# A decode step on one core: TensorE loops tile by tile, and the softmax runs in groups of six and two blocks

## The chip, the cores and the metric

One core of one Trainium2 chip. The time is the device time of one execution, in microseconds (us), as the median of several runs. The kernel before ran at 1293.13 us (three runs, 1293.12 to 1293.23). The profile is one execution, with its own span of 1291.9 us. The time does not start and end with the profile's span and is 1.3 to 1.5 us longer, so spans are compared with spans and times with times.

## The reference

One step of attention over a long cache, plus a small MLP, for 8 sequences:

```python
q = (xn @ wq)                          # xn = layernorm(x): 8 x 576; 32 heads of 128
scores = einsum(q, k_cache) * 128**-0.5   # k_cache, v_cache: 8 x 32 x 4096 x 128, bf16
o = einsum(softmax(scores), v_cache) @ wo
h = gelu(layernorm(xn) @ w1 + b1)      # 576 -> 4608
out = x + o + h @ w2 + b2
```

The two caches are 268 MB each and every byte is used once. Everything else together is about 20 MB.

## The kernel before

The caches pass through a ring in SBUF in 32 tiles. A tile is 128 partitions: eight heads of one sequence, 16 partitions a head, 256 keys in each partition. One tile has one key load and one value load of 8.39 MB each, both issued by SyncE on one queue:

```python
for t in range(1, NT):
    sy.wait_ge(sem["kf"], 2 * t - 1)   # TensorE has read enough of the old keys
    load_kv(k_v, t, 0)
    sy.wait_ge(sem["vf"], t)           # TensorE has read the old values
    load_kv(v_v, t, 1)
```

VectorE multiplies each of eight key blocks by the query in place, TensorE adds up groups of 16 columns with identity matmuls, and VectorE reduces the rest to scores. The softmax is done in two halves of four blocks. `spread_heads` turns the exponentials into matmul weights `ebd`:

```python
def vector_tile(t, u):
    ve.wait_ge(sem["k"], 16 * (u + 1))
    for x in range(NX):                     # NX = 8 blocks
        ...                                 # product of block x, in place
        if x > 1:
            reduce(u, x - 2)
        if x == NCB + 2:                    # after product 6
            spread_heads(u, 0)              # first half of the softmax
    reduce(u, NX - 2)
    reduce(u, NX - 1)
    spread_heads(u, 1)                      # second half
    ...                                     # reciprocal, scaling, result
```

TensorE's program has two tiles written out in one loop of 16 turns (64 product matmuls, 64 value matmuls, two totals, four transposes of the result in each tile); the first of the totals signals `vf`:

```python
with nc.Fori(0, NT // 2, 1, engines=[ENG.DVE, ENG.PE, ENG.Activation]) as it:
    for u in range(2):
        vector_tile(2 * it + u, u)
        tensor_tile(u)
        scalar_tile(u)
```

The softmax here doesn't subtract the row's maximum and nothing guards it: scores larger than these inputs give would overflow.

## Time and profile before

| | kernel before |
|---|---|
| time | 1293.13 us |
| HBM bytes read | 556.94 MB |
| from one load's completion to the next, steady | 19.35 us (433.5 GB/s) |
| a tile (two loads) | 38.70 us, without change |
| TensorE, VectorE busy | 60%, 64% |

The first excerpt is from the page of the kernel before. The row `DMA` is the busy share of the 16 DMA engines in 40 slices of the span, in tenths; the queue lines (`q1`, `q8`) give packets, MB and their share of the engines' time; the group lines give busy time and the mean of one instruction in ns, then the engine's idle time just before them and what ended it; the last two lines give the number of issues and the median time from issue to landing.

```profile
PE 770.1 (60%) x4780; PEld 318.3 (25%) x4780; DVE 828.1 (64%) x708; ACT 56.6 (4%) x181; POOL 1.4 (0%) x11
...
DMA  9999999999999999999999999999999999999998
...
q1 hardware_dynamic: 10368, 556.93, 99.7%
q8 instruction: 4, 0.07, 0.0%
...
DMA 82%; PE 11%; DVE 6%; issue 0%; ACT 0%; DVEq 0%; SPq 0%
...
L524 DVE TENSOR_TENSOR ring<-ring,qb 128x4096 bf16<-128x4096 bf16 x256 | 579.8, 2286 | 239.6 <-DMA ring<-in_A_k_cache_dram 239.3
...
ring<-in_A_k_cache_dram SPq DMA_DIRECT2D x32, 32.2
ring<-in_A_v_cache_dram SPq DMA_DIRECT2D x32, 29.4
```

Read it from the DMA row: it is 9 nearly throughout, while no compute engine is above 64%. A load takes 19.35 us on the wire but 32.2 or 29.4 us from issue to landing, so each one waits 10 to 13 us in the queue behind the one before. That is what a full queue looks like.

The next excerpt is the chain of waits of the kernel before: start, length, what.

```profile
556.52 32.16 DMA ring<-in_A_k_cache_dram
...
588.83 2.30 DVE ring L524
...
591.18 4.04 PE s_ps L552 x9
...
595.23 32.15 DMA ring<-in_A_k_cache_dram
```

The chain runs through the key load and then through 2.3 us of VectorE and 4 us of TensorE before the next key load is issued. This looks like 6 us of compute per tile on the path (the page sums it to 17%), but it is not: the load issued at 595.2 us only joins a queue in which the value load is still being moved. The chain follows the releaser of each step; it does not know that the DMA engines were busy with something else meanwhile. The completion times of the packets do: they come 19.35 us apart with no hole.

The excerpt is the timeline of the end of one tile in the kernel before (start, length, engine, line, operation, tiles, and in brackets the idle time before it); weight loads are left out.

```profile
571.87 1.29 DVE L506 TENSOR_REDUCE sc<-s_ps 128x32 f32<-128x512 f32 x2
...
573.85 1.91 PE L563 MATMUL o_ps<-ring,ebd 128*32 128x512 bf16 x32
...
575.11 1.23 DVE L514 TENSOR_TENSOR ebd<-e,head 128x1024 bf16<-128x1024 bf16 x1 [0.47 <-ACT e L582]
...
576.39 1.91 PE L563 MATMUL o_ps<-ring,ebd 128*32 128x512 bf16 x32 [0.64 <-DVE ebd L514]
...
578.65 0.33 SPq L246 DMA_DIRECT2D ring<-in_A_v_cache_dram  x1
...
580.49 0.19 DVE L541 TENSOR_TENSOR Ox<-on,quad 128x32 bf16 x1
588.83 2.29 DVE L524 TENSOR_TENSOR ring<-ring,qb 128x4096 bf16<-128x4096 bf16 x1 [8.15 <-DMA ring<-in_A_k_cache_dram]
```

The last product has ended at 571.9 us. The second half of the softmax follows (reduce, exp, spread), then the second half of the value matmuls, and the value load is released at 578.65 us. The tile's work ends at 580.7 us, and VectorE then waits 8.15 us for the next keys.

### The profile page before, as it was taken

The page shows a single profiled execution, that of the slowest core. Times are in us where ns is not written, and L with a number is a line of the kernel's source. Part 1 is how long each engine was busy: PE and PEld are TensorE (multiplying, and loading weights), DVE is VectorE, ACT ScalarE, POOL GpSimd, SP SyncE. Part 2 cuts the span into 40 slices and gives each one's busy share as a digit, 9 for nine tenths or more (in the row PEclk, how much of TensorE's full clock was granted, in tenths as well). Part 3 has the DMA queues.
Part 4 walks back from the last instruction along what each step waited for, and adds up shares of the span by engine and source line. Part 5 has one row for each costly group of instructions (what it writes and reads, how often), then busy time and mean ns, then how long its engine had stood idle before and what let it go on. Part 6 is the DMA issues. An engine that isn't in the chain of part 4 may idle for free.

```text
span 1291.9 us, 10994 instructions
## 1 busy us (share of the span) xinstructions
PE 770.1 (60%) x4780; PEld 318.3 (25%) x4780; DVE 828.1 (64%) x708; ACT 56.6 (4%) x181; POOL 1.4 (0%) x11
## 2 busy tenths in 40 slices
PE   5665675655665654675565575555565655675567
PEld 1122222222221222222222222222222222222223
DVE  2655677655677655677655677655677655577654
ACT  2100000000000000000000000000000000000000
POOL 0000000000000000000000000000000000000000
PEclk9877887777887777887778887777887777887779
DMA  9999999999999999999999999999999999999998
GB/s 415 445 425 443 428 428 444 426 428 446 424 430 444 426 432 442 426 432 440 428 442 428 428 444 426 428 446 424 430 444 428 430 442 426 432 440 428 442 428 352
DMA packets 10411, 557.03 MB, mean 431 GB/s; under 512 B 1163, under 2 KB 1188, under 8 KB 1446
## 3 DMA queue, kind: packets, MB, share of 16 engines
q1 hardware_dynamic: 10368, 556.93, 99.7%
q8 instruction: 4, 0.07, 0.0%
q10 hardware_dynamic: 38, 0.02, 0.0%
q14 instruction: 1, 0.01, 0.0%
HBM read 556.94 MB, written 0.01 MB: 431 GB/s over the span
## 4 chain that ended last, share of the span: by engine, by line
DMA 82%; PE 11%; DVE 6%; issue 0%; ACT 0%; DVEq 0%; SPq 0%
DMA ring<-in_A_k_cache_dram 77%; PE s_ps L552 10%; DVE ring L524 6%; DMA ring<-in_A_wo_dram 2%; DMA ring<-in_B_w_dram 2%; PE o_ps L387 1%; PE s_ps L387 1%; DVEq L524 0%; PE acc L347 0%; ACT L401 0%; DVE ring L404 0%; ACT ring L401 0%; DVE ring L402 0%; DVE ring L400 0%; ACT ring L397 0%
## 5 line engine op out<-in xcount | busy, mean ns | idle before, releaser
L552 PE MATMUL s_ps<-ring,ident 128*128 128x512 bf16 x2048 | 555.3, 429 | 477.5 <-DVE ring L524 476.6
L524 DVE TENSOR_TENSOR ring<-ring,qb 128x4096 bf16<-128x4096 bf16 x256 | 579.8, 2286 | 239.6 <-DMA ring<-in_A_k_cache_dram 239.3
L552 PEld LDWEIGHTS s_ps<-ring,ident 128*128 128x128 bf16 x2048 | 205.9, 107 | 808.8 <-DVE ring L524 549.5
L506 DVE TENSOR_REDUCE sc<-s_ps 128x32 f32<-128x512 f32 x256 | 173.1, 687 | 37.8 <-PE s_ps L552 37.8
L563 PE MATMUL o_ps<-ring,ebd 128*32 128x512 bf16 x2048 | 129.9, 401 | 13.5 <-DVE ebd L514 13.4
L514 DVE TENSOR_TENSOR ebd<-e,head 128x1024 bf16<-128x1024 bf16 x64 | 78.2, 1223 | 15.0 <-ACT e L582 15.0
L563 PEld LDWEIGHTS o_ps<-ring,ebd 128*32 128x32 bf16 x2048 | 50.9, 101 | 95.5 <-issue 30.7
L582 ACT ACTIVATE e<-sc 128x128 bf16<-128x128 f32 x64 | 19.9, 311 | 1080.2 <-DVE sc L506 1080.2
L535 DVE RECIPROCAL rec<-tot_ps 128x8 f32<-128x8 f32 x32 | 6.7, 208 | 82.1 <-PE tot_ps L569 82.1
L575 PE MATMUL oT_ps<-selc,ob 128*128 128x8 f32 x256 | 33.9, 259 | 5.2 <-ACT ob L586 5.2
L575 PEld LDWEIGHTS oT_ps<-selc,ob 128*128 128x128 f32 x256 | 31.0, 191 | 8.1 <-ACT ob L586 8.1
L538 DVE TENSOR_TENSOR on<-oT_ps,rec 128x8 bf16<-128x8 f32 x32 | 5.3, 167 | 34.7 <-PE oT_ps L575 34.7
L586 ACT ACTIVATE ob<-o_ps 128x512 f32<-128x512 f32 x32 | 19.1, 597 | 105.5 <-PE o_ps L563 105.5
L569 PEld LDWEIGHTS tot_ps<-headf,Ep 128*128 128x128 f32 x128 | 16.6, 188 | 13.6 <-issue 13.6
L569 PE MATMUL tot_ps<-headf,Ep 128*128 128x8 f32 x128 | 19.6, 261 | 0.0
L398 DVE TENSOR_SCALAR ring<-ring 96x384 f32<-96x384 f32 x2 | 0.7, 353 | 25.8 <-ACT ring L397 25.8
L582 ACT ACTIVATION_READ_ACCUMULATOR e<-sc 128x1 f32 x64 | 12.0, 187 | 0.0
L387 PE MATMUL o_ps<-ring 128*32 128x384 bf16 x27 | 7.9, 862 | 2.4 <-DMA ring<-in_B_w_dram 2.4
L541 DVE TENSOR_TENSOR Ox<-on,quad 128x32 bf16 x32 | 6.2, 193 | 4.8
L387 PE MATMUL s_ps<-ring 128*32 128x384 bf16 x27 | 7.9, 863 | 0.0
L347 PE MATMUL acc<-ring,hT_sb 128*8 128x288 bf16 x72 | 6.4, 350 | 1.7 <-DMA ring<-in_B_w_dram 1.7
L295 PE MATMUL tot_ps<-ident,ring 8*128 8x8 bf16 x9 | 0.7, 198 | 8.9 <-DVE ring L288 8.9
(77 smaller groups left out, 58.0 us busy)
## 6 DMA issues: line engine op xcount, KB each, us to landing
ring<-in_B_w_dram SPq DMA_DIRECT2D x2, 5184.0 KB, 25.4
ring<-in_A_wq_dram SPq DMA_DIRECT2D x1, 4608.0 KB, 13.8
ring<-in_A_wo_dram SPq DMA_DIRECT2D x1, 1728.0 KB, 28.9
ring<-in_A_wo_dram SPq DMA_DIRECT2D x1, 1584.0 KB, 28.9
ring<-in_A_wo_dram SPq DMA_DIRECT2D x1, 1008.0 KB, 30.9
ring<-in_A_k_cache_dram SPq DMA_DIRECT2D x32, 32.2
ring<-in_A_v_cache_dram SPq DMA_DIRECT2D x32, 29.4
ring<-in_A_wo_dram SPq DMA_DIRECT2D x1, 288.0 KB, 31.1
```

The lines of the kernel that those rows point to most:

```text
L347: i = e.matmul(acc[m][m * OP:m * OP + B, :ND], lhsT=lhsT, rhs=rhs[:, m * ND:(m + 1) * ND], start=start, stop=stop)
L387: i = e.matmul(h_ps[j][s * MP:(s + 1) * MP], lhsT=lhsT, rhs=wv[:, r0:r0 + HK, :], **flags)
L506: ins = ve.tensor_reduce(out=sc[i][:, n * CB:(n + 1) * CB], in_=bank_of(x).rearrange("p (c d) -> p c d", d=DL), axis=AX.X, op=ALU.add)
L514: ve.tensor_tensor(out=ebd[i][:], in0=es[i][:].rearrange("p (j c) -> p j c", c=4).unsqueeze(2).to_broadcast([P, J, G, 4]), in1=head[:].uns ...
L524: ve.tensor_tensor(out=k, in0=k, in1=qb[:, bass.ds(t, 1), :].to_broadcast([P, CB, Dh]), op=ALU.mult,).then_inc(sem["prod"], 1)
L535: ve.reciprocal(out=rec[:], in_=tot_ps[:, :G]).then_inc(sem["rec"], 1)
L552: ins = te.matmul(bank_of(x).rearrange("p (c d) -> p c d", d=DL), lhsT=idn, rhs=k[:, :, d * DL:(d + 1) * DL], start=(d == 0), stop=(d == n ...
L563: ins = te.matmul(o_ps[m * MP:(m + 1) * MP, :], lhsT=ebd[i][:, j].rearrange("p g c -> p (g c)"), rhs=ring_v[u][i][:, 4 * j:4 * j + 4, :], ...
L569: ins = te.matmul(tot_ps[:, :G], lhsT=Ep[:, i:i + 1].to_broadcast([P, P]), rhs=headf[:], start=(i == 0), stop=(i == 1))
L575: ins = te.matmul(oT_ps[:, :G], lhsT=ob[:, c, :], rhs=selc[:, c, :], start=(c == 0), stop=(c == 3))
L582: sa.activation(out=es[i][:], in_=sc[i][:], func=ACT.Exp, scale=scale, accum_out=Ep[:, i:i + 1]).then_inc(sem["x"], 1)
L586: sa.activation(out=ob[:].rearrange("r c d -> r (c d)"), in_=o_ps, func=ACT.Copy).then_inc(sem["ob"], 1)
```

## The change

Its intent, in its author's words: TensorE loops tile by tile, with two product sections and one values section, so that its program is 1021 instructions; and the softmax runs in groups of six and two blocks. The core of the diff (cuts marked):

```diff
-    HALVES = [(1, 0), (0, 1)]
+    BLOCKS = [(7, 0, 1, 2, 5, 6, 3, 4), (0, 1, 2, 5, 6, 7, 3, 4)]
+    LATE = 2
+    groups = [(0, NX - LATE), (NX - LATE, NX)]
 ...
         for x in range(NX):
+            if x == NX - 1:
+                reduce(u, x - 2)
 ...                                        # product of block x
-            if x > 1:
+            if 1 < x < NX - 1:
                 reduce(u, x - 2)
-            if x == NCB + 2:
-                spread_heads(u, 0)
+        spread_heads(u, 0)
         reduce(u, NX - 2)
         reduce(u, NX - 1)
         spread_heads(u, 1)
 ...
-    with nc.Fori(0, NT // 2, 1, engines=[ENG.DVE, ENG.PE, ENG.Activation]) as it:
+    with nc.Fori(0, NT // 2, 1, engines=[ENG.DVE, ENG.Activation]) as it:
 ...
+    block("even")
+    nc.regs_mov(odd, 0)
+    products(0)
+    te.br("values")
+    block("odd")
+    nc.regs_mov(odd, 1)
+    products(1)
+    te.br("values")
+    block("values")
 ...                                        # 64 value matmuls, one total, four transposes
+    turn_end(te, prod=NX, v=16, ebd=2, ob=1)
+    te.br_lt(odd, 1, on_true="odd", on_false="turn")
+    block("turn")
+    nc.regs_alu(turns, turns, 1, op=ALU.add)
+    te.br_lt(turns, NT // 2, on_true="even", on_false="project")
```

Besides this, the two small transposes of the head are merged into one of nine matmuls, and VectorE adds the two rows of softmax totals so that one totals matmul is left per tile. The bytes moved and the point at which key blocks are released do not change.

More of the change, by code (lines that the diff above doesn't have):

```diff
@@ L36, in __init__ @@
         self.sems, self.counts, self.seen, self.bufs = {}, {}, {}, {}
+        self.aside = []
     def buf(self, key):
@@ L49, in wait @@
         if self.seen.get((eng, sem.num), 0) < value:
-            getattr(self.nc, eng).wait_ge(sem, value)
             self.seen[eng, sem.num] = value
+            if eng == "tensor":
+                self.aside.append(lambda: self.nc.tensor.wait_ge(sem, value))
+            else:
+                getattr(self.nc, eng).wait_ge(sem, value)
     def deps(self, eng, reads, writes):
@@ L67, in op @@
             self.wait(eng, token)
-        ins = emit(getattr(self.nc, eng))
         if sem is None:
@@ L71, in op @@
             self.counts[eng] += 1
-            value = self.counts[eng]
-            ins.then_inc(sem, 1)
-            token = (eng, (sem, value))
+            token = (eng, (sem, self.counts[eng]))
         else:
-            ins.then_inc(sem, 16)
             token = ("dma", (sem, 16))
+        if eng == "tensor":
+            self.aside.append(lambda: emit(self.nc.tensor).then_inc(sem, 1))
+        else:
+            ins = emit(getattr(self.nc, eng))
+            ins.then_inc(sem, 1 if token[0] == eng else 16)
+            self.name = ins.ins.name
         for key in reads:
@@ L82, in op @@
             b.writer, b.readers = token, []
-        self.name = ins.ins.name
         return token[1]
@@ L106, in ahead, with later @@
     bb.instructions = rest[:at] + moved + rest[at:]
+def later(src, dst, engine):
+    ins = list(src.instructions)
+    wait = next(i for i in ins if i.engine == engine and type(i).__name__ == "InstEventSemaphore")
+    assert not dst.instructions
+    src.instructions = [i for i in ins if i is not wait]
+    dst.instructions = [wait]
 def decode(nc, A_x, A_k_cache, A_v_cache, A_wq, A_wo, B_x, B_w1, B_b1, B_w2, B_b2, out):
@@ L155, in decode @@
     qb = sb("qb", [P, NT, Dh], BF16)
-    ebd = [sb(f"ebd{i}", [P, J, G, 4], BF16) for i in range(2)]
-    sc = [sb(f"sc{i}", [P, CH], FP32) for i in range(2)]
-    es = [sb(f"e{i}", [P, CH], BF16) for i in range(2)]
+    ebd = sb("ebd", [P, 2 * J, G, 4], BF16)
+    sc = sb("sc", [P, C], FP32)
+    es = sb("es", [P, C], BF16)
     Ep = sb("Ep", [P, 2], FP32)
+    Es = sb("Es", [P, 1], FP32)
     ob = sb("ob", [P, 4, Dh], FP32)
@@ L207, in decode @@
     xn8, y8 = early(0, [B, D]), early(0, [B, D])
-    dup = early(0, [B, D, 2])
+    YP = 32
+    dup = early(0, [YP + B, D, 2])
     xT = early(0, [P, WC, MP])
@@ L226, in decode, with block @@
     od = Order(nc)
+    main = nc.cur_bb
+    def block(name, eng=ENG.PE):
+        nc.enter_bb(name, parent=main, valid_engines=[eng])
     wq_sb = ring[:, 0:WQ_END].rearrange("p (c f) -> p c f", c=WC)
@@ L258, in decode @@
     od.op("gpsimd", [], ["eps"], lambda e: e.memset(eps_col[:], EPS))
+    od.op("gpsimd", [], ["dup"], lambda e: e.memset(dup, 0.0))
     od.op("gpsimd", [], ["xT"], lambda e: e.memset(xT, 0.0))
@@ L285, in layernorm, with spread @@
             op0=ALU.subtract, op1=ALU.mult))
-    def spread(src, skey, dst, dkey, ps, pkey):
+    def spread(src, skey, p0):
         dve([skey], ["dup"], lambda e: e.tensor_copy(
-            out=dup, in_=src.unsqueeze(2).to_broadcast([B, D, 2])))
-        dupv = dup.rearrange("b d v -> b (d v)").rearrange("b (p c) -> b c p", c=WC)
-        tp = ps[:, :WC * B].rearrange("p (c b) -> p c b", c=WC)
-        def turn(e):
-            for c in range(WC):
-                i = e.matmul(
-                    tp[:, c, :], lhsT=dupv[:, c, :], rhs=ident[:B, :B], start=True, stop=True)
-            return i
-        pe(["dup", "ident"], [pkey], turn)
-        for v in range(2):
-            dve([pkey, "par"], [dkey], lambda e: e.tensor_tensor(
-                out=dst[:, :, v * B:(v + 1) * B], in0=tp,
-                in1=par[:, :, v:v + 1].to_broadcast([P, WC, B]), op=ALU.mult))
+            out=dup[p0:p0 + B], in_=src.unsqueeze(2).to_broadcast([B, D, 2])))
     layernorm(x8, "x8", xn8, "xn8", "x")
@@ L313, in decode, with turn_both @@
             in_=par2[:, 1 - v:2 - v].unsqueeze(1).to_broadcast([P, WC // 2, 1])))
-    spread(xn8, "xn8", xT, "xT", tot_ps, "tot")
+    spread(xn8, "xn8", 0)
     layernorm(xn8, "xn8", y8, "y8", "y")
-    spread(y8, "y8", yT, "yT", oT_ps, "oT")
+    spread(y8, "y8", YP)
     idn = ident[:]
+    dupv = dup.rearrange("b d v -> b (d v)").rearrange("b (p c) -> b c p", c=WC)
+    tp = tot_ps[:, :WC * 2 * B].rearrange("p (c t b) -> p c t b", c=WC, t=2)
+    two = idn[:YP + B, :2 * YP].rearrange("p (t i) -> p t i", t=2)[:, :, :B]
+    def turn_both(e):
+        for c in range(WC):
+            i = e.matmul(tp[:, c], lhsT=dupv[:, c, :], rhs=two, start=True, stop=True)
+        return i
+    pe(["dup", "ident"], ["tot"], turn_both)
+    for t, (dst, dkey) in enumerate(((xT, "xT"), (yT, "yT"))):
+        for v in range(2):
+            dve(["tot", "par"], [dkey], lambda e: e.tensor_tensor(
+                out=dst[:, :, v * B:(v + 1) * B], in0=tp[:, :, t],
+                in1=par[:, :, v:v + 1].to_broadcast([P, WC, B]), op=ALU.mult))
     act(["ident"], ["sel"], lambda e: e.activation(
@@ L362, in decode, with broadcast @@
         t = ps.rearrange("p (g d) -> p g d", d=Dh)
-        def broadcast(e):
+        def broadcast(e, t=t, b=b):
             for v in range(2):
@@ L391, in decode @@
     for c in range(WC):
-        pe(["yT", "w1"], ["h_ps"], lambda e: layer(
+        pe(["yT", "w1"], ["h_ps"], lambda e, c=c: layer(
             e, yT[:, c, :], w1_sb[:, c, :], start=(c == 0), stop=False))
@@ L408, in decode, with turn @@
         t = S_ps[j][:, :HK * HS * MP].rearrange("p (k n) -> p k n", k=HK)
-        def turn(e):
+        def turn(e, h=h, t=t):
             for k in range(HK):
@@ L454, in decode @@
         sy.dma_start(out=wo_rows(r0, r1), in_=wo_v[:, r0 * D:r1 * D]).then_inc(wo_in[-1], 16)
-    HALVES = [(1, 0), (0, 1)]
-    def block(u, x):
-        i, n = divmod(x, NCB)
-        return HALVES[u][i], (n + NCB - 1) % NCB if u == 0 and i == 0 else n
+    BLOCKS = [(7, 0, 1, 2, 5, 6, 3, 4), (0, 1, 2, 5, 6, 7, 3, 4)]
+    SLOTS = BLOCKS[1]
+    LATE = 2
+    assert len(SLOTS) == NX and all(b[-LATE:] == SLOTS[-LATE:] for b in BLOCKS)
+    groups = [(0, NX - LATE), (NX - LATE, NX)]
     def keys(u, x):
-        h, n = block(u, x)
-        at = home(u, 0) + h * CHUNK + n * BLOCK
+        at = home(u, 0) + BLOCKS[u][x] * BLOCK
         return ring[:, at:at + BLOCK].rearrange("p (c d) -> p c d", d=Dh)
-    ring_v = [[ring[:, h * CHUNK:(h + 1) * CHUNK].rearrange("p (c d) -> p c d", d=Dh)
-               for h in HALVES[u]] for u in range(2)]
+    vals = ring[:, :TILE].rearrange("p (c d) -> p c d", d=Dh)
     def bank_of(x):
@@ L500, in decode, with turn_end @@
         od.wait("tensor", od.last(e))
+    def turn_end(e, **counts):
+        for name, n in counts.items():
+            e.wait_ge(sem[name], n).then_inc(sem[name], -n)
     def reduce(u, x):
-        i, m = divmod(x, NCB)
-        n = block(u, x)[1]
+        n = SLOTS.index(BLOCKS[u][x])
         ve.wait_ge(sem["s"], NX * u + x + 1)
         ins = ve.tensor_reduce(
-            out=sc[i][:, n * CB:(n + 1) * CB],
+            out=sc[:, n * CB:(n + 1) * CB],
             in_=bank_of(x).rearrange("p (c d) -> p c d", d=DL), axis=AX.X, op=ALU.add)
-        if m == NCB - 1:
+        if x + 1 in (groups[0][1], NX):
             ins.then_inc(sem["sc"], 1)
     def spread_heads(u, i):
+        a, b = (n * CB for n in groups[i])
+        ja, jb, nj = a // 4, b // 4, (b - a) // 4
         ve.wait_ge(sem["x"], 2 * u + i + 1)
+        if i:
+            ve.tensor_tensor(out=Es[:], in0=Ep[:, 0:1], in1=Ep[:, 1:2], op=ALU.add)
         ve.tensor_tensor(
-            out=ebd[i][:],
-            in0=es[i][:].rearrange("p (j c) -> p j c", c=4).unsqueeze(2).to_broadcast([P, J, G, 4]),
-            in1=head[:].unsqueeze(1).unsqueeze(3).to_broadcast([P, J, G, 4]), op=ALU.mult,
+            out=ebd[:, ja:jb],
+            in0=es[:, a:b].rearrange("p (j c) -> p j c", c=4).unsqueeze(2)
+            .to_broadcast([P, nj, G, 4]),
+            in1=head[:].unsqueeze(1).unsqueeze(3).to_broadcast([P, nj, G, 4]), op=ALU.mult,
         ).then_inc(sem["ebd"], 1)
@@ L533, in vector_tile @@
         spread_heads(u, 1)
-        ve.wait_ge(sem["t"], 2 * u + 1)
+        ve.wait_ge(sem["t"], u + 1)
         ve.reciprocal(out=rec[:], in_=tot_ps[:, :G]).then_inc(sem["rec"], 1)
         ve.wait_ge(sem["rec"], 2 * u + 1)
-        ve.wait_ge(sem["t"], 2 * u + 2)
         ve.tensor_tensor(
@@ L544, in vector_tile, with scalar_tile, products @@
             in1=quad[:].unsqueeze(1).to_broadcast([P, G, M]), op=ALU.mult).then_inc(sem["on"], 1)
-    def tensor_tile(u):
+    def scalar_tile(u):
+        for i, (a, b) in enumerate(groups):
+            sa.wait_ge(sem["sc"], 2 * u + i + 1)
+            sa.activation(
+                out=es[:, a * CB:b * CB], in_=sc[:, a * CB:b * CB], func=ACT.Exp, scale=scale,
+                accum_out=Ep[:, i:i + 1]).then_inc(sem["x"], 1)
+        sa.wait_ge(sem["o"], u + 1)
+        sa.activation(
+            out=ob[:].rearrange("r c d -> r (c d)"), in_=o_ps, func=ACT.Copy
+        ).then_inc(sem["ob"], 1)
+    te.br("head")
+    assert NT % 2 == 0
+    with nc.Fori(0, NT // 2, 1, engines=[ENG.DVE, ENG.Activation]) as it:
+        for u in range(2):
+            vector_tile(2 * it + u, u)
+            scalar_tile(u)
+        turn_end(ve, k=32, s=2 * NX, x=4, t=2, rec=4)
+        turn_end(sa, sc=4, o=2)
+    ve.wait_ge(sem["end"], 1)
+    ve.tensor_copy(
+        out=OT[:], in_=S_ps[0][:, :RO * B].rearrange("p (r b) -> p r b", b=B)).then_inc(sem["on"], 1)
+    ve.wait_ge(sem["end"], 2)
+    ve.tensor_copy(out=fin[:B], in_=acc[0][:B, :ND]).then_inc(fin_d, 1)
+    sa.wait_ge(sem["end"], 2)
+    sa.activation(
+        out=fin[OP:OP + B], in_=acc[1][OP:OP + B, :ND], func=ACT.Copy).then_inc(fin_a, 1)
+    sa.wait_ge(fin_a, 1)
+    sa.dma_start(out=out2[:, ND:], in_=fin[OP:OP + B]).then_inc(sem["out"], 16)
+    sa.sem_inc(sent)
+    def products(u):
         for x in range(NX):
-            te.wait_ge(sem["prod"], NX * u + x + 1)
+            te.wait_ge(sem["prod"], x + 1)
             k = keys(u, x)
@@ L557, in tensor_tile @@
             ins.then_inc(sem["s"], 1)
-        te.wait_ge(sem["v"], 16 * (u + 1))
-        for i in range(2):
-            te.wait_ge(sem["ebd"], 2 * u + i + 1)
-            for j in range(J):
-                m = j % M
-                ins = te.matmul(
-                    o_ps[m * MP:(m + 1) * MP, :], lhsT=ebd[i][:, j].rearrange("p g c -> p (g c)"),
-                    rhs=ring_v[u][i][:, 4 * j:4 * j + 4, :],
-                    start=(i == 0 and j < M), stop=(i == 1 and j >= J - M))
-        ins.then_inc(sem["o"], 1)
@@ L568, in tensor_tile @@
-        for i in range(2):
-            ins = te.matmul(
-                tot_ps[:, :G], lhsT=Ep[:, i:i + 1].to_broadcast([P, P]), rhs=headf[:],
-                start=(i == 0), stop=(i == 1))
-            ins.then_inc(sem["t" if i else "vf"], 1)
-        te.wait_ge(sem["ob"], u + 1)
-        for c in range(4):
-            ins = te.matmul(
-                oT_ps[:, :G], lhsT=ob[:, c, :], rhs=selc[:, c, :], start=(c == 0), stop=(c == 3))
-        ins.then_inc(sem["t"], 1)
-    def scalar_tile(u):
-        for i in range(2):
-            sa.wait_ge(sem["sc"], 2 * u + i + 1)
-            sa.activation(
-                out=es[i][:], in_=sc[i][:], func=ACT.Exp, scale=scale, accum_out=Ep[:, i:i + 1]
-            ).then_inc(sem["x"], 1)
-        sa.wait_ge(sem["o"], u + 1)
-        sa.activation(
-            out=ob[:].rearrange("r c d -> r (c d)"), in_=o_ps, func=ACT.Copy
-        ).then_inc(sem["ob"], 1)
@@ L590, in turn_end @@
-    def turn_end(e, **counts):
-        for name, n in counts.items():
-            e.wait_ge(sem[name], n).then_inc(sem[name], -n)
-    assert NT % 2 == 0
-    with nc.Fori(0, NT // 2, 1, engines=[ENG.DVE, ENG.PE, ENG.Activation]) as it:
-        for u in range(2):
-            vector_tile(2 * it + u, u)
-            tensor_tile(u)
-            scalar_tile(u)
-        turn_end(ve, k=32, s=2 * NX, x=4, t=4, rec=4)
-        turn_end(sa, sc=4, o=2)
-        turn_end(te, prod=2 * NX, v=32, ebd=4, ob=2)
+    block("head")
@@ new lines, in decode @@
+    for emit in od.aside:
+        emit()
+    turns = nc.alloc_registers("turns", engines=[ENG.PE])
+    odd = nc.alloc_registers("odd", engines=[ENG.PE])
+    nc.regs_mov(turns, 0)
+    te.br("even")
+    block("even")
[7 more added lines that the diff above has]
+    block("values")
+    te.wait_ge(sem["v"], 16)
+    for i, (a, b) in enumerate(groups):
+        te.wait_ge(sem["ebd"], i + 1)
+        for j in range(a * J // NCB, b * J // NCB):
+            m = j % M
+            c = SLOTS[j * NCB // J] * CB + 4 * j % CB
+            ins = te.matmul(
+                o_ps[m * MP:(m + 1) * MP, :], lhsT=ebd[:, j].rearrange("p g c -> p (g c)"),
+                rhs=vals[:, c:c + 4, :], start=(j < M), stop=(j >= 2 * J - M))
@@ new lines, in decode @@
+    ins.then_inc(sem["o"], 1)
+    te.matmul(tot_ps[:, :G], lhsT=Es[:].to_broadcast([P, P]), rhs=headf[:], start=True, stop=True
+              ).then_inc(sem["vf"], 1)
+    te.wait_ge(sem["ob"], 1)
+    for c in range(4):
+        ins = te.matmul(
+            oT_ps[:, :G], lhsT=ob[:, c, :], rhs=selc[:, c, :], start=(c == 0), stop=(c == 3))
+    ins.then_inc(sem["t"], 1)
+    turn_end(te, prod=NX, v=16, ebd=2, ob=1)
+    te.br_lt(odd, 1, on_true="odd", on_false="turn")
+    block("turn")
+    nc.regs_alu(turns, turns, 1, op=ALU.add)
@@ L604, in decode @@
+    te.br_lt(turns, NT // 2, on_true="even", on_false="project")
+    block("project")
     parts = [(v, r) for v in range(2) for r in range(R)]
@@ L619, in decode @@
     ins.then_inc(sem["end"], 1)
-    ve.wait_ge(sem["end"], 1)
-    ve.tensor_copy(
-        out=OT[:], in_=S_ps[0][:, :RO * B].rearrange("p (r b) -> p r b", b=B)).then_inc(sem["on"], 1)
     hidden_part()
@@ L631, in decode @@
     ins.then_inc(sem["end"], 1)
-    ve.wait_ge(sem["end"], 2)
-    ve.tensor_copy(out=fin[:B], in_=acc[0][:B, :ND]).then_inc(fin_d, 1)
-    sa.wait_ge(sem["end"], 2)
-    sa.activation(
-        out=fin[OP:OP + B], in_=acc[1][OP:OP + B, :ND], func=ACT.Copy).then_inc(fin_a, 1)
-    sa.wait_ge(fin_a, 1)
-    sa.dma_start(out=out2[:, ND:], in_=fin[OP:OP + B]).then_inc(sem["out"], 16)
-    sa.sem_inc(sent)
 _INS = ['A_x', 'A_k_cache', 'A_v_cache', 'A_wq', 'A_wo', 'B_x', 'B_w1', 'B_b1', 'B_w2', 'B_b2']
```

## The prediction

> **What bounds the kernel now.** The DMA engines. The page counts 556.94 MB over a 1291.9 us span; the 40-slice DMA row shows 9 nearly throughout, while PE is busy 60% and DVE 64%. In the records of DMA packets, consecutive 8.39 MB cache loads complete 19.35 us apart, without change from the third tile to the last: 433.5 GB/s, with no hole. A tile (one key load, one value load) is 38.70 us. The queue never runs dry: the issue table gives 32.2 us (keys) and 29.4 us (values) from issue to landing against 19.35 us of transfer, so each waits 10 to 13 us behind its predecessor. In the timeline the tile's compute ends at 502.8 us and DVE then idles 8.15 us until the next keys land. The end is DMA too: the last output-weight rows land at 1288.9, PE finishes 1.3 us later, and copy and store end by 1291.5.
>
> **What the change does.**
> - TensorE loops once per tile instead of once per two; the merged turns drop 9 matmuls and the summed row totals one. Its program falls from about 1190 (my count, two instructions per matmul) to 1021.
> - DVE: the first weights multiply (1.22 us for half the softmax) moves behind the last product and covers 6 of 8 blocks (estimate 1.8 us), and the second shrinks to about 0.65 us. The last product moves 1.1 us earlier, and only two blocks' reduce, exp and multiply follow it. The value matmuls and so the next value load start an estimated 1.5 to 2 us earlier per tile. No bytes and no key releases change.
> - Head: queries now also wait for the second layernorm, ready at an estimated 13 us; they start at 13.96 because wq lands then. No delay. An extra memset (about 1.2 us by the existing ones) is done well before it is read.
>
> **What lies on the critical path.** The softmax and value rearrangement does not: 2 us earlier values only lengthen the wait in the DMA queue (issue to landing of values: 29.4 to about 31). DVE idle before the keys grows.
>
> One small thing does. The queue table shows 4 instruction packets; their records are 16,384 B each, about 1.0 us long, at 27.7, 73.9, 104.7 and 1282.5 us[...]. [...] Each holds up one of the 16 engines, which never catches up because the queue is never empty: the spread from median to last engine is 0.54 us at the first load's completion, 1.89 us from the fifth on, until the end. [...]
>
> **Prediction.** 1293.1 minus 0.8: 1292.3 us; 8 in 10 between 1291.5 and 1293.3. Faster by over 2%: 0.5%; within: 99%; slower: 0.5%.
>
> **What would show it.** Tile period still 38.70 us; value issue-to-landing 1 to 2 us longer; DVE idle before keys about 1 us longer; 16 KiB instruction packets fewer than 4; last-engine spread below 1.89 us if none remain early; last landing before 1288.9 by as much as the time falls.
>
> **What would make it wrong.** [...] a value load issued over 9 us late would open a hole; PE late at the end (it had 0.9 us of idle before the last rows) would eat the gain.

Terms are cut from this record, marked there. What they came to is the 0.8 us that the forecast takes off 1293.1 us: the author's estimate for fewer instruction packets during the run, between nothing and about 1.3 us (the growth of the last engine's spread from 0.54 to 1.89 us).

## The result, and the profile after

| | before | after |
|---|---|---|
| time, median of six runs | 1293.09 us (1293.04 to 1293.23) | 1293.05 us (1293.01 to 1293.24) |
| span of the profiled run | 1291.9 us | 1291.7 us |
| last load landed | 1288.93 us | 1288.68 us |
| a tile | 38.70 us | 38.70 us |
| value load issued before the first DMA engine is done with the keys ahead of it, median of tiles 5 to 32 | 7.33 us (least 5.68) | 9.17 us (least 9.16) |
| 16 KiB instruction packets | 4 | 4 |

The verdict is "same": ratio 1.0, with a 95% interval of 0.9987 to 1.0013. Ratios are the mean time of one kernel's fast runs over that of the other's of the same rounds, so not quite the ratio of the medians quoted.

The page of the kernel after, the same lines:

```profile
PE 730.1 (57%) x4707; PEld 306.8 (24%) x4707; DVE 827.0 (64%) x740; ACT 56.7 (4%) x181; POOL 2.4 (0%) x12
...
DMA  9999999999999999999999999999999999999998
...
q1 hardware_dynamic: 10368, 556.93, 99.7%
q8 instruction: 4, 0.07, 0.0%
...
DMA 82%; PE 11%; DVE 6%; issue 0%; ACT 0%; DVEq 0%; SPq 0%
...
L557 DVE TENSOR_TENSOR ring<-ring,qb 128x4096 bf16<-128x4096 bf16 x256 | 578.8, 2282 | 288.7 <-DMA ring<-in_A_k_cache_dram 288.7
...
ring<-in_A_k_cache_dram SPq DMA_DIRECT2D x32, 32.2
ring<-in_A_v_cache_dram SPq DMA_DIRECT2D x32, 30.7
```

TensorE is 40 us less busy and VectorE waits 49 us longer for keys (288.7 against 239.3). The value loads take 30.7 us from issue to landing instead of 29.4. The queue of key loads, the bytes and the DMA row are as they were. The chain of waits has the same three steps of the same length:

```profile
556.27 32.16 DMA ring<-in_A_k_cache_dram
...
588.58 2.30 DVE ring L557
...
590.93 4.04 PE s_ps L617 x9
...
594.98 32.15 DMA ring<-in_A_k_cache_dram
```

The end of the same tile in the kernel after:

```profile
571.08 1.75 DVE L544 TENSOR_TENSOR ebd<-es,head 128x1536 bf16<-128x1536 bf16 x1
...
572.75 1.28 DVE L532 TENSOR_REDUCE sc<-s_ps 128x32 f32<-128x512 f32 x2
...
573.05 3.64 PE L646 MATMUL o_ps<-ring,ebd 128*32 128x512 bf16 x64
...
574.52 0.68 DVE L544 TENSOR_TENSOR ebd<-es,head 128x512 bf16<-128x512 bf16 x1
...
577.03 0.33 SPq L269 DMA_DIRECT2D ring<-in_A_v_cache_dram  x1
...
579.04 0.19 DVE L572 TENSOR_TENSOR Ox<-on,quad 128x32 bf16 x1
588.58 2.29 DVE L557 TENSOR_TENSOR ring<-ring,qb 128x4096 bf16<-128x4096 bf16 x1 [9.34 <-DMA ring<-in_A_k_cache_dram]
```

VectorE spreads six blocks right after the last product (1.75 us), only two blocks' reduce, exp and spread (0.68 us) follow, and the 64 value matmuls run in one go. The value load is issued at 577.03 us instead of 578.65. VectorE then waits 9.34 us for its keys and takes them up at 588.58 us (588.83 before). The gain of the change is all in this wait.

### The profile page after: what moved, and what is told of

Read it like the earlier page. It is cut to its first block, busy times and chain, and to the rows that moved or that the text cites. A ratio compares the mean times of both kernels' runs of the same rounds, so it can differ in the third digit from the quotient of the medians.

```text
span 1291.7 us, 10993 instructions
## 1 busy us (share of the span) xinstructions
PE 730.1 (57%) x4707; PEld 306.8 (24%) x4707; DVE 827.0 (64%) x740; ACT 56.7 (4%) x181; POOL 2.4 (0%) x12
## 4 chain that ended last, share of the span: by engine, by line
DMA 82%; PE 11%; DVE 6%; issue 0%; ACT 0%; DVEq 0%; SPq 0%
DMA ring<-in_A_k_cache_dram 78%; PE s_ps L617 10%; DVE ring L557 6%; DMA ring<-in_A_wo_dram 2%; DMA ring<-in_B_w_dram 2%; PE o_ps L412 1%; PE s_ps L412 1%; DVEq L557 0%; PE acc L372 0%; ACT L426 0%; DVE ring L429 0%; ACT ring L426 0%; DVE ring L427 0%; DVE ring L425 0%; ACT ring L422 0%
## 5 line engine op out<-in xcount | busy, mean ns | idle before, releaser
L617 PE MATMUL s_ps<-ring,ident 128*128 128x512 bf16 x2048 | 537.4, 418 | 520.0 <-DVE ring L557 520.0
L557 DVE TENSOR_TENSOR ring<-ring,qb 128x4096 bf16<-128x4096 bf16 x256 | 578.8, 2282 | 288.7 <-DMA ring<-in_A_k_cache_dram 288.7
L617 PEld LDWEIGHTS s_ps<-ring,ident 128*128 128x128 bf16 x2048 | 201.9, 106 | 842.8 <-DVE ring L557 594.2
L532 DVE TENSOR_REDUCE sc<-s_ps 128x32 f32<-128x512 f32 x256 | 169.0, 680 | 0.0
L646 PE MATMUL o_ps<-ring,ebd 128*32 128x512 bf16 x2048 | 116.4, 380 | 0.0
L544 DVE TENSOR_TENSOR ebd<-es,head 128x1536 bf16<-128x1536 bf16 x64 | 77.8, 1216 | 0.0
L580 ACT ACTIVATE es<-sc 128x192 bf16<-128x192 f32 x64 | 19.8, 310 | 1109.9 <-DVE sc L532 1109.9
L543 DVE TENSOR_TENSOR Es<-Ep 128x1 f32<-128x1 f32 x32 | 5.1, 160 | 13.3 <-ACT es L580 13.3
L650 PEld LDWEIGHTS tot_ps<-headf,Es 128*128 128x128 f32 x64 | 9.5, 186 | 13.6 <-issue 13.6
L650 PE MATMUL tot_ps<-headf,Es 128*128 128x8 f32 x64 | 12.4, 266 | 0.0
L580 ACT ACTIVATION_READ_ACCUMULATOR es<-sc 128x1 f32 x64 | 11.9, 186 | 0.0
## 6 DMA issues: line engine op xcount, KB each, us to landing
ring<-in_A_wo_dram SPq DMA_DIRECT2D x1, 1584.0 KB, 29.2
ring<-in_A_v_cache_dram SPq DMA_DIRECT2D x32, 30.7
```

The lines of the kernel that those rows point to most:

```text
L532: ins = ve.tensor_reduce(out=sc[:, n * CB:(n + 1) * CB], in_=bank_of(x).rearrange("p (c d) -> p c d", d=DL), axis=AX.X, op=ALU.add)
L544: ve.tensor_tensor(out=ebd[:, ja:jb], in0=es[:, a:b].rearrange("p (j c) -> p j c", c=4).unsqueeze(2) .to_broadcast([P, nj, G, 4]), in1=hea ...
L557: ve.tensor_tensor(out=k, in0=k, in1=qb[:, bass.ds(t, 1), :].to_broadcast([P, CB, Dh]), op=ALU.mult,).then_inc(sem["prod"], 1)
L580: sa.activation(out=es[:, a * CB:b * CB], in_=sc[:, a * CB:b * CB], func=ACT.Exp, scale=scale, accum_out=Ep[:, i:i + 1]).then_inc(sem["x"], 1)
L617: ins = te.matmul(bank_of(x).rearrange("p (c d) -> p c d", d=DL), lhsT=idn, rhs=k[:, :, d * DL:(d + 1) * DL], start=(d == 0), stop=(d == n ...
L646: ins = te.matmul(o_ps[m * MP:(m + 1) * MP, :], lhsT=ebd[:, j].rearrange("p g c -> p (g c)"), rhs=vals[:, c:c + 4, :], start=(j < M), stop ...
```

## The experiments

The theory: the DMA queue is never empty, so work per tile can shrink or grow, within a limit, without moving the time. The rivals: the two parts of the change cancel each other; TensorE's work matters; or the new kernel lost to instruction packets what it gained.

**1. The loop alone.** The changed kernel with the softmax in halves again:

```diff
-    BLOCKS = [(7, 0, 1, 2, 5, 6, 3, 4), (0, 1, 2, 5, 6, 7, 3, 4)]
-    LATE = 2
+    BLOCKS = [(7, 0, 1, 2, 3, 4, 5, 6), (0, 1, 2, 7, 3, 4, 5, 6)]
+    LATE = 4
 ...
+            if x == NCB + 2:
+                spread_heads(u, 0)
 ...
-        spread_heads(u, 0)
```

> The changed kernel with the softmax put back into two halves, the first spread before the last product, as in the kernel before: the TensorE loop alone. Theory (the DMA queue is never empty, so neither part is on the path): 1293.0 us, within 0.3; value loads again 29 to 30 us from issue to landing instead of 30.7; still 4 instruction packets. Rival (the two parts cancel: the per-tile branches cost what the softmax gains): slower than the kernel before by 1 us or more, up to 1.7 us for each of 32 tiles.

Measured: 1293.07 us (1293.00 to 1293.14), before 1293.14 in the same rounds; ratio 1.0 (0.9986 to 1.0013). One line of its page:

```profile
ring<-in_A_v_cache_dram SPq DMA_DIRECT2D x32, 29.2
```

**2. The softmax alone.** The changed kernel with TensorE's loop written out over two tiles again (1159 TensorE instructions by my count of the built program; the same count gives 1010 for the changed kernel, not the 1021 of its author, and 1178 for the kernel before). In short:

```diff
-    products(0); te.br("values") ... products(1); te.br("values") ... block("values")
+    for u in range(2):
+        products(u)
+        values()
```

> The changed kernel with the TensorE loop unrolled over two tiles again: the softmax grouping alone, a program of about 1170 instructions. Theory: 1293.0 us, within 0.3; value loads 30 to 31 us from issue to landing; 4 instruction packets, three of them before 110 us. Rival (the parts cancel): faster than the kernel before by 1 us or more.

Measured: 1293.14 us (1292.93 to 1293.18), before 1293.14; ratio 0.9999 (0.9986 to 1.0013).

```profile
ring<-in_A_v_cache_dram SPq DMA_DIRECT2D x32, 30.7
```

Neither part alone moves the time, so they do not cancel. The longer wait of the value loads comes from the softmax grouping alone: 30.7 us with it, 29.2 to 29.4 without. TensorE's loop form shows nowhere in these numbers, and the branches in each tile bring no further instruction packets: the pages of both kernels count 4. With the softmax alone three of them came before 110 us (32.6, 73.8 and 107.4 us), as expected.

The lead of the value loads on the first DMA engine that is done with the keys is a finer measure. On average over tiles 5 to 32 it is 6.9 us in the kernel before, 6.9 us with the loop alone, 8.7 us with the softmax alone and 9.2 us with both. So the softmax grouping gains 1.7 us on top of the old loop, 2.2 us on top of the new one.

**3. TensorE stripped.** Wrong on purpose (relative error 0.71): one product matmul per block (two in the two blocks that release keys), four value matmuls per tile, the head and the projection cut alike; waits and loads all stay. The program is 194 instructions:

```diff
-            for d in range(nd):
+            for d in range(2 if x in (1, 3) else 1):
 ...
-        for j in range(a * J // NCB, b * J // NCB):
+        for j in range(a * J // NCB, a * J // NCB + 2):
 ...                                     # head, hidden layer and projection likewise
```

> Wrong on purpose: one product matmul per block instead of eight, four value matmuls per tile instead of 64, the head and the projection cut alike; every wait and every DMA stays. The TensorE program is about 200 instructions[...]. Theory: TensorE busy falls from 730 us to under 150 us and the time falls by no more than the lag of the last DMA engine, to 1291.3 to 1292.2 us, with no 16 KiB instruction packet before the last microseconds and a spread of the last engine over the median under 0.6 us instead of 1.6. Rival (TensorE's work, 11% of the chain of waits, matters): tens of us faster.

Measured: 1292.88 us (1292.47 to 1293.50), before 1293.14; ratio 0.9997 (0.9984 to 1.0011).

```profile
span 1291.3 us, 3218 instructions
...
PE 306.5 (24%) x819; PEld 111.6 (9%) x819; DVE 827.2 (64%) x740; ACT 56.2 (4%) x181; POOL 2.4 (0%) x12
...
q1 hardware_dynamic: 10368, 556.93, 99.7%
q10 hardware_dynamic: 38, 0.02, 0.0%
q14 instruction: 1, 0.01, 0.0%
...
ring<-in_A_v_cache_dram SPq DMA_DIRECT2D x32, 31.4
```

TensorE lost over half its busy time and the time stayed. (It kept more than the expected 150 us: 819 matmuls in 306.5 us are 374 ns each, against 155 ns in the changed kernel, 730.1 us by 4707. The trace shows single matmuls of 128x512 at 0.61 us (mean of 320) where eight in a row took 1.90 us in the changed kernel.) That rules out TensorE's work as a limit, in spite of the 11% that the chain of waits gives it. The page has no line for 16 KiB instruction packets (the others show `q8`); in the records one begins 1292.7 us after the span's start, which is after its end. But the expected gain of 1 us did not come either: the median time fell by 0.26 us, within the interval. The spans of the five runs (1290.8 to 1291.3 us) are about 0.7 us shorter than those of the kernel before (1291.6 to 1291.9 us); the rest of the time, outside the span, was longer here (1.4 to 2.4 us, against 1.3 to 1.4), and why is not shown. The records of DMA packets show where the lag came from. The spread, the time from the median of the 16 engines to the last one at the completion of a load, was (loads in order: the query weights, the first MLP weights, then keys and values in turn; in us):

```
load                      1st   3rd   4th   5th   7th   65th  last landing
before                    0.54  1.51  1.54  1.90  1.89  1.89  1288.93
after                     0.34  1.58  1.59  1.61  1.60  1.57  1288.68
TensorE stripped          0.50  0.50  1.29  1.30  1.33  1.49  1288.49
```

In both real kernels the 16 KiB packet at 27.7 or 30.2 us (1.00 and 1.02 us long; the cache packet after it takes 2.89 us instead of 2.42) sets the third load's last engine back by about 1 us, for good. Without it, the third load's spread stays 0.50. Then the spread jumps to 1.29 at the fourth load. An 8 KiB instruction packet on another queue starts at 49.716 us, between the two completions. The records do not name the engine, but an engine's packets follow one another without a gap (in both real kernels each packet of 65,536 B from 30 to 1270 us starts within 0.02 us of the end of another), and only one cache packet ends there, at 49.720 us. The instruction packet lasts 0.31 us; at its end, at 50.022 us, the next cache packet starts, and it takes 3.03 us where its neighbours take 2.42. So one engine, until then the second to last (0.15 us ahead of the last), lost 0.92 us and is now the last. The same packet is there at 52 us in both real kernels too, where it did not set the maximum. The slow rise from 1.29 to 1.49 us after it, with no further instruction packet, is not explained.

**4. A longer program.** The changed kernel with 1024 more TensorE instructions ahead of the head, each a wait on a semaphore that is long set:

```diff
+    for _ in range(2048):            # two waits become one instruction
+        te.wait_ge(od.sem("gpsimd"), 1)
     for emit in od.aside:
```

> The changed kernel with 1024 TensorE instructions that only wait on a semaphore that is long set, put ahead of the head[...]. Theory of the fetches: 8 packets of 16 KiB instead of 4, four of them in the first 15 us, each about 1 us on one of 16 DMA engines; the time grows by 0 to 2 us, with the spread of the last engine (1.0 to 1.2 us more for each further fetch that falls on the engine that is already last). Rival (the fetches do not lag the engines): same spread, same time.

Measured: 1382.47 us (1381.40 to 1384.16), ratio 1.0692. It missed, because TensorE started late: it stood in the padding for over 100 us. (The page counts 12017 instructions, 1024 more than that of the changed kernel.) Whether the waits themselves take that time or the instruction packets do is not separated here. One line of its waits (engine, tile, what ended the idle time; us in total, times, longest):

```profile
PE tot_ps L334 <- issue: 112.4, 1, 112.4
```

TensorE needed 112.4 us for the padding, about 0.11 us an instruction with whatever the instruction packets add, so the first value load was issued late: the third load was complete at 46 us and the fourth at 145 us, about 80 us of empty queue. What it does show is the number of 16 KiB packets, by the queue lines of its page: 8, as expected, but the first four came over the padding, 24 to 28 us apart (27.5 to 106.8 us), and not within 15 us. And after the empty queue the spread was back at 0.29 us (fourth load); it was 1.32 and 2.64 us at the next two, with instruction packets at 145.2 and 168.6 us, and stayed 2.6 us to the end. The queue was still filling up then, so this agrees with the lag but does not isolate it; what excludes the rival that these packets do not lag an engine is the third load of experiment 3.

**5. Delay in each tile.** Both kernels with R repeats of the last block's reduce, into a scratch tile, ahead of the last reduce (8 took 4.87 us, 11 took 6.66, 14 took 8.47):

```diff
         reduce(u, NX - 2)
+        ve.wait_ge(sem["s"], NX * u + NX)
+        for n in range(R):
+            ve.tensor_reduce(out=idle[:, n], in_=bank_of(NX - 1)..., axis=AX.X, op=ALU.add)
         reduce(u, NX - 1)
```

> The kernel before, with 14 repeats of the last block's reduce into a scratch tile ahead of the last reduce, about 8.4 us per tile of pure delay before the value load is released. Theory: from keys landing to the end of the tile's work took 30.9 us, now 39.3 us, over the 38.7 us of transfer per tile: 1305 to 1320 us. Rival (the softmax change is worth nothing in itself): as slow or fast as the changed kernel with the same delay.

> The changed kernel with the same 14 repeats. Theory: the tile's work took 29.5 us, now 37.9 us, still under 38.7 us: 1293 us, at most 1300. If it is the kernel before that stays at 1293 and this one that grows, the theory of the slack is wrong.

> The kernel before with 18 repeats, about 10.8 us per tile. Theory: 41.7 us of work per tile, now the longer of the two: about 1385 us.

> The changed kernel with 18 repeats. Theory: 40.3 us of work per tile: about 1340 us, 45 to 55 us faster than the kernel before with the same delay, that is 1.4 to 1.7 us for each of 32 tiles. Rival: the same as the kernel before with the delay.

Then, with a better estimate of the room (its "half clock": in the changed kernel with 14 repeats, 48 value matmuls took 2.77 us, and the last 16, after 7.81 us of idle time, 1.90 us):

> The kernel before with 11 repeats (11 x 0.6 = 6.6 us). With 14 repeats (8.47 us measured) the two kernels took 41.5 and 40.0 us per tile, which leaves 32.6 to 33.0 and 31.5 us of own work per tile, TensorE's half clock after the idle stretch included; so the room under 38.7 us is about 6 us before and 7.2 us after. Theory: 39.3 us per tile here, 1300 to 1325 us. Rival (the room is the same in both kernels): the same time as the changed kernel with 11 repeats.

> The changed kernel with 11 repeats (6.6 us). Theory: 38.1 us of own work per tile, still under 38.7: 1293 us, at most 1297. If it grows like the kernel before with the same delay, the room is not larger after the change.

> The kernel before with 8 repeats (4.8 us). Theory: 37.6 us of own work per tile, under 38.7 even in the kernel before: 1293 us, at most 1296. If it grows by tens of us, the tile's work is on the path without any delay and the theory of the full DMA queue is wrong.

| R | before | after | value load issued, against the first DMA engine done with its keys (median of tiles 5 to 32; minus is ahead): before, after |
|---|---|---|---|
| 0 | 1293.09 us | 1293.05 us | -7.33, -9.17 us |
| 8 | 1316.41 us | not run | -1.18 us |
| 11 | 1358.01 us | 1298.95 us | +0.42, -2.03 us |
| 14 | 1369.67 us | 1334.58 us | +0.69, -0.89 us |
| 18 | 1481.54 us | 1399.24 us | +4.14, +1.62 us |

The direction is as the theory has it: with the same delay the changed kernel is 35 us faster at 14 repeats, 59 us at 11 and 82 us at 18. At 11 the interval for the changed kernel is 1.0028 to 1.0059 of the kernel before without delay, run in the same rounds, and for the kernel before 1.049 to 1.0522. So the change is worth something in itself, and a full queue hides it. The sizes missed: the changed kernel with 14 repeats should have stayed at 1293, and the kernel before should have borne 8. With 8 it grew by 23 us (ratio 1.0165 to 1.0206), and the expectation above says that growth by tens of us would refute the full queue. So that test, as it was written, went against the theory; what follows saves it after the fact, from the traces. Two things were left out of my sums. The first is the clock. The timeline of the kernel before with 8 repeats:

```profile
581.45 1.42 PEld L569 LDWEIGHTS o_ps<-ring,ebd 128*32 128x32 bf16 x32 [0.42 <-issue]
...
581.55 4.87 DVE L535 TENSOR_REDUCE idle<-s_ps 128x32 f32<-128x512 f32 x8 [0.80 <-PE s_ps L558]
...
588.77 3.61 PE L569 MATMUL o_ps<-ring,ebd 128*32 128x512 bf16 x32 [5.42 <-DVE ebd L515]
...
592.79 0.33 SPq L247 DMA_DIRECT2D ring<-in_A_v_cache_dram  x1
...
594.56 0.19 DVE L547 TENSOR_TENSOR Ox<-on,quad 128x32 bf16 x1
599.18 2.29 DVE L525 TENSOR_TENSOR ring<-ring,qb 128x4096 bf16<-128x4096 bf16 x1 [4.42 <-DMA ring<-in_A_k_cache_dram]
```

The delay leaves TensorE idle for 5.42 us between the two halves, and the second 32 value matmuls then take 3.61 us where the first take 1.91. The granted clock is 0.89 from 581 to 587 us and 0.54 from 587 to 593 us. (Without a delay it is 0.50 from 584 to 590 us, where TensorE is idle between tiles.) How short an idle stretch is enough was not tested. So a delay of 4.87 us became 6.15 us (-7.33 to -1.18). The changed kernel has only 16 matmuls after the delay (at 11 repeats):

```profile
575.00 2.77 PE L652 MATMUL o_ps<-ring,ebd 128*32 128x512 bf16 x48
575.29 6.66 DVE L567 TENSOR_REDUCE idle<-s_ps 128x32 f32<-128x512 f32 x11
...
583.78 1.90 PE L652 MATMUL o_ps<-ring,ebd 128*32 128x512 bf16 x16 [6.01 <-DVE ebd L545]
...
586.24 0.33 SPq L270 DMA_DIRECT2D ring<-in_A_v_cache_dram  x1
```

They take 1.90 us, as long as 32 take before the idle stretch. So part of the difference between the delayed kernels is that 16 instead of 32 matmuls run at the lower clock. The second thing left out is what the queue needs: in the table, a value load issued 2.03 us ahead of the first engine's completion costs 0.2 us a tile (38.89 against 38.70), and one issued 1.18 us ahead costs 0.8 us (39.46). The single tiles of the kernel before with 8 repeats show the same: the ten value loads issued 1.98 to 3.04 us ahead completed at most 0.27 us late, those issued 0 to 0.5 us ahead 1.0 to 1.7 us late (median engine). Where the queue had run dry, the first packet of a value load started 0.95 us after its issue (1.00 us at the start of the kernel before, where the queue was still empty: 0.09 and 1.09 us). So a lead of about 2 us is needed, against the first engine of the 16 and not the last. The room is then about 5 us in the kernel before and about 7 us in the changed one.

**6. The tail.** The changed kernel with the output weights in five loads, to see if the end gives what the loop can't:

```diff
-    CUTS = (0, 12, 23, 30, RO)
+    CUTS = (0, 12, 23, 27, 30, RO)
```

> The changed kernel with the output weights cut into five loads instead of four (the third one, seven rows, into four and three), to see if the tail can give what the loop could not: 18 matmuls (1.27 us) now start when the third load has landed at 1288.4, 0.24 us before the last. Theory: 0 to 0.5 us less than the changed kernel, since the fourth row group waits for nearly the same last engine; within 2% in any case.

Measured: 1293.24 us (1292.87 to 1293.36), before 1293.12; ratio 1.0 (0.9986 to 1.0014). TensorE's last matmuls end at 1289.8 us (timeline; 1289.7 in the changed kernel), so the finer cut gains nothing. No version with a right result was clear of both kernels.

## Why the prediction was right or wrong

- **DMA bounds the kernel: right.** The period of a tile is 38.70 us before, after, and in both halves of the change. Taking away over half of TensorE's busy time left the time the same (0.9984 to 1.0011). (The prediction's 502.8 us for the end of a tile's work should read 503.3; nothing rests on it.)
- **The softmax gives 1.5 to 2 us a tile, off the path: right, and shown.** Value loads were issued 1.84 us earlier against the DMA engines (7.33 to 9.17 us) with both parts of the change (medians; the averages give 2.2 us, and 1.7 us with the softmax alone). They took 30.7 us from issue to landing (predicted about 31), VectorE's idle time before the keys grew by 1.2 us in the tile shown (predicted about 1), and the delays of experiment 5 brought the gain to light.
- **The head costs nothing: right.** The queries started at 13.89 us (13.96 before) and the first product at 46.88 us (47.06 before).
- **The 0.8 us for fewer instruction packets: this is the step that failed, in number and in worth.** Four packets remained: at 30.2, 73.5, 271.9 and 1287.1 us, instead of 27.7, 73.9, 104.7 and 1282.5. I reckoned that the program of 1021 would need at least one packet less. But the last packet starts when about 970 instructions of the program have run: in both traces, 206 matmuls and weight loads are left of 1178 instructions before, and 38 of 1010 after, so the shorter program passed the point just before it ended. And the worth itself was mis-sized: with no 16 KiB packet at all during the run (experiment 3) the last landing was at 1288.49 us, 0.44 us earlier than before and not the estimated 1.3, since another instruction packet of 8 KiB set back an engine. (That is one trace; the spans of the five runs are 0.7 us shorter on average.) The third packet, at 271.9 us, does not fit the step either: by then the loop had run all its code several times, so it did not come with a first pass through the code. The point of 1292.3 us was 0.75 us too low: the forecast gain did not come. The range held by its width: its upper end stood 0.2 us above the old time.
- **The branches in each tile bring no instruction packets: right.** 32 tiles of branches, four packets. The kernel before jumps back 15 times over two tiles' 560 matmuls and weight loads, and from 104.7 us, in its first turn, to 1282.5 us no 16 KiB packet falls.
- **"A value load issued over 9 us late would open a hole": too generous.** The room was about 5 us before and 7 us after, because TensorE's clock falls when it idles (0.89 to 0.54 around an idle stretch of 5.42 us) and because the load must be issued about 2 us ahead of the first engine (2.03 us ahead cost 0.2 us a tile, 1.18 us ahead 0.8), which is done about 2 us before the last (2.3 and 1.8 us, medians of the kernel before and after).

What stays open: why the third packet comes at 271.9 us in the changed kernel, at 160.4 us in the loop-only version and at 114.5 us in that of experiment 6, whose programs have the same length (one trace each); why an engine's next cache packet takes 0.5 to 0.6 us longer after an instruction packet; and what the 8 KiB packet at 52 us is for.

## What to carry to other kernels

When every load waits 10 us in a full DMA queue, as here, work taken out of the tile only lengthens that wait; read the time from issue to landing against the transfer time before costing anything else. The chain of waits may still show 17% of compute, because it follows releasers and not the queue. To find out how much room a hidden improvement buys, put the same delay into both kernels: here 6.66 us a tile cost 65 us in one and 6 us in the other.
